# One condition for both matrices of a new expert, split by two engines, and one condition around the tail

## The chip, the cores and the metric

The program runs on one core of a Trainium2 chip. A core has TensorE (PE, matrix products; its weight loads are shown as PEld), VectorE (DVE), ScalarE (ACT), GpSimd (POOL) and SyncE (SP, which here issues most transfers). Each engine works through a list of its own in order and waits for the others by semaphores. The metric is the device time of one execution in microseconds (us). Three runs of the kernel before took 1461.64, 1463.62 and 1466.49 us; the median is 1463.62.

## The reference

Three stages follow each other: an attention with 32 landmarks, a mixture of eight experts of which each row takes one, and a feed-forward stage with a squared rectifier.

```python
x = attention(q, k, v)                       # 4608 rows of 512
logits = x @ w_gate; e = argmax(logits)      # one of 8 experts per row, gate_w its probability
for e in range(8):                           # w1[e] 512 x 1024, w2[e] 1024 x 512
    out[e's rows] = gate_w * (maximum(x[e's rows] @ w1[e], 0) @ w2[e])
h = maximum(out @ w_in, 0)                   # 512 x 2048
return (h * h) @ w_out                       # 2048 x 512
```

## The kernel before, in words

Only the middle stage, phase_m1, and its ends are touched. The rows were sorted by expert into tiles of 128 rows; tiles 0 and 1 are done earlier. The loop (from L1024) is written out for tiles 2 to 44, since 45 tiles would be needed for the worst distribution of rows; how many there are, `nt`, is known only on the chip. Tiles 36 (`NTF`) to 44 stand therefore each in a condition of its own, `tc.If(nt > j)` at L1031. A condition is a branch on every engine; the side that is not taken holds the instructions that bring each semaphore to the value it would have had, on POOL one INC_SWDGE_SEM for the tile's transfers.

A float32 matrix is held as the sum of two float16 matrices, a high and a low part, and each product is made of three: high by high, high by low, low by high. A tile `j` is one call of `step(j)`:

- mm1 in two halves of 48 matmuls each (L120 to L122): rows times w1. After each half ACT writes the high part of the hidden tile hT (L125) and DVE the low part (L126).
- mm2, 24 matmuls (L135): hT times w2. Its first four need the high part of the first half of hT, its next four the low part.
- post: the result is scaled and split (L143, L149, L157) and scattered by POOL (L158); prep of tile j + 2 (L56 to L94): the same for rows that POOL gathered (L80).
- the transpose of the next tile's rows, which SP issues as a transfer at the top of the step (L108) and which that tile's mm1 waits for.
- a part of a fill: one of 32 pieces of the last stage's weights, loaded by SP (L1055) and split by ACT, DVE and, for the second matrix, POOL (L1068 to L1095).

The experts' weights lie in `wb` (split) and the next expert's in `stg` (float32, 2 MB for each of w1 and w2). `change(j, i)` stands once for each matrix: `change(j, 0)` at the end of step j - 1, behind mm2, and `change(j, 1)` in step j between the two halves of mm1. Each has a condition (L966): where tile j begins a new expert, `conv` splits the staged matrix in four quarters, three by ACT (high, L1040) and DVE (low, L1049), one by POOL alone (L1042, L1046, L1047). Behind each condition SP issues the load of the matrix of the expert after that (L951), which does nothing where none is needed. With this input 38 tiles exist, and tiles 9, 14, 23 and 28 begin a new expert.

The last stage, phase_m2, takes blocks of 256 rows. Per block there are eight pairs: 24 matmuls (L1137 to L1139), then ACT, five DVE instructions on a tile `q` of eight slots, ACT and DVE again (L1142 to L1149). The products (L1161) of a block begin when the next block's second pair is out.

Of the kernel before, what the change touches and what calls it, by code (L numbers as in the profile page):

```python
# [6 lines left out]
F32 = mybir.dt.float32  # L7
# [19 lines left out]
NTL = 45  # L27
# [908 lines left out]
def phase_m1(tc, cst, x_rows, x2, w1, w2, rt, stg, wb, fill, first):  # L936
    nc = tc.nc
    identh = cst["identh"]
    with (
        tc.tile_pool(name="m1", bufs=1, reuse_waits="tile") as m1,  # L940
        tc.tile_pool(name="m2", bufs=2, reuse_waits="tile") as m2,
        tc.tile_pool(name="m3", bufs=3, reuse_waits="tile") as m3,
        tc.tile_pool(name="m5", bufs=5, reuse_waits="tile") as m5,
        tc.tile_pool(name="mph", bufs=2, space=PSUM, reuse_waits="tile") as mph,
        tc.tile_pool(name="mpy", bufs=2, space=PSUM, reuse_waits="tile") as mpy,
    ):
        st = [dict() for _ in range(NTL)]
# [14 lines left out]

        def change(j, i):

            s = st[j]
            with tc.If((chw[j // 16] >> (j % 16)) & 1):  # L966
                conv(nc, stg, wb, m2, i)
            load(s["nx"], s["ld"], i)

        pools = dict(xg=m3, xm=m3, s1=m5, xh=m2, gt=m5, xT=m2, hT=m1, yg=m1, ym=m3, s2=m3, ss=m3, xr=m2,  # L970
                     ph=mph, py=mpy)
# [18 lines left out]
        run(L.turn(st[PT]))  # L990
        change(PT, 0)
        idle = iter(())
# [5 lines left out]
        def step(j):  # L998
# [11 lines left out]
            run(L.mm1(st[j], 0))  # L1010
            change(j, 1)
            if j + 3 < NTL:
# [5 lines left out]
            if not last:  # L1018
                change(j + 1, 0)
            go(fl, old, pr, fl)  # L1020
            if j + 1 >= NTF:
                go(*(4 * [L.post(st[j], rt["sidx"][:, j:j + 1], rt["gidx"][:, j:j + 1])]))

        for j in range(PT, NTL):  # L1024
            if j + 2 < NTL:
                regs(j + 2)
            if j < NTF:
                step(j)
            else:

                with tc.If(nt > j):  # L1031
                    step(j)


def conv(nc, stg, wb, pool, i):

    for c in (3, 0, 1, 2):
        cs = slice(1024 * c, 1024 * c + 1024)
        if c < 3:
            nc.scalar.activation(wb[:, i, 0, cs], stg[:, i, cs], AF.Copy, scale=128.0)  # L1040
        if c == 3:
            nc.gpsimd.tensor_scalar(wb[:, i, 0, cs], stg[:, i, cs], 128.0, 1.0, op0=ALU.mult, op1=ALU.mult)  # L1042
            for h in range(2):
                hs = slice(cs.start + 512 * h, cs.start + 512 * h + 512)
                t = pool.tile([128, 512], F32, tag="cv", name="cv", bufs=1)
                nc.gpsimd.tensor_scalar(t, stg[:, i, hs], 128.0, 1.0, op0=ALU.mult, op1=ALU.mult)  # L1046
                nc.gpsimd.tensor_tensor(wb[:, i, 1, hs], t, wb[:, i, 0, hs], op=ALU.subtract)  # L1047
        else:
            nc.vector.scalar_tensor_tensor(wb[:, i, 1, cs], stg[:, i, cs], 128.0, wb[:, i, 0, cs],  # L1049
                                           op0=ALU.mult, op1=ALU.subtract)  # L1050

# [7 lines left out]
def wide_split(tc, pool, w, scale, dst, quad=None):  # L1059
# [17 lines left out]
    if quad is None:  # L1077
        to = c = g.bitcast(F32)
    else:
        if quad[1] == 0:  # L1080
            quad[0].append(pool.tile([128, 8, 256], F32, tag="fq", name="fq", bufs=1))
        c = quad[0][0]
        to = c[:, 4 + 2 * (1 - quad[1]):6 + 2 * (1 - quad[1])].rearrange("p s n -> p (s n)")
    V.scalar_tensor_tensor(to.bitcast(I32), hi, -0x80000000, g, op0=ALU.bitwise_and, op1=ALU.bitwise_or)
    if quad is not None:
        if quad[1] == 0:
            return

# [13 lines left out]

PRODS = ((6, 6, 0), (4, 4, 2), (1, 1, 0), (0, 0, 1), (2, 2, 0), (5, 3, 0), (3, 5, 1))

# [13 lines left out]
def phase_m2(tc, x2, wi, wo, wb, first, out):  # L1118
# [4 lines left out]
    with (  # L1123
# [7 lines left out]
        def pair(xT, hq, i):  # L1131
# [8 lines left out]

            q = n3.tile([128, 8, 128], F32, tag="q", name="q")
            ACT.activation(q[:, 4:8], ph.rearrange("p z (t n) -> p (z t) n", t=2), AF.Relu, scale=2.0 ** -7)  # L1142
            V.tensor_tensor(q[:, 4:8], q[:, 4:8], q[:, 4:8], op=ALU.mult)  # L1143
            V.tensor_tensor(q[:, 0], q[:, 7], q[:, 5], op=ALU.add)  # L1144
            V.tensor_tensor(q[:, 2], q[:, 6], q[:, 7], op=ALU.subtract)  # L1145
            V.tensor_tensor(q[:, 1], q[:, 0], q[:, 6], op=ALU.subtract)  # L1146
            V.tensor_tensor(q[:, 3], q[:, 4], q[:, 1], op=ALU.subtract)  # L1147
            ACT.activation(hq[:, 0, i], q[:, 0:7], AF.Copy, scale=0.5)  # L1148
            V.scalar_tensor_tensor(hq[:, 1, i], q[:, 0:7], 0.5, hq[:, 0, i], op0=ALU.mult, op1=ALU.subtract)  # L1149

# [140 lines left out]
```

## Time and profile before

| | us |
|---|---|
| median of three runs | 1463.62 |
| the profiled execution | 1462.96 |
| its span, from the first to the last instruction | 1461.3 |
| PE busy in the span | 1351.2 (92%) |
| DVE busy | 1020.3 (70%) |
| ACT busy | 569.7 (39%) |
| POOL busy | 319.6 (22%) |

All durations below are from the profiled execution, of which 1.7 us lie outside the span. The expert stage runs from about 287 to 717.5 us, the last stage from 736.2 us to the end. A tile of the expert stage is the stretch from its first mm1 matmul to the next tile's.

### The profile page before, as it was taken

Reading aid. Unit: us, or ns where it says so; the run is one execution under the profiler, and the core shown is the slowest. Engines: PE = TensorE matmul, PEld = TensorE weight load, DVE = VectorE, ACT = ScalarE, POOL = GpSimd, SP = SyncE. Lnnn points to the kernel's source line nnn. Section 1 sums busy time; section 2 is a strip of 40 time slices with the busy share of each in tenths; the row PEclk is TensorE's granted clock in tenths of the full one; section 3 lists DMA queues with packets and bytes.
Section 4 is the critical chain, followed back from the end, with each engine's and each line's share of the span. In section 5 each row is a group of like instructions: output and inputs, shape, how many; then the busy total and the mean of one; then the engine's idle time right before and its main releaser. Section 6 shows DMA issues by size and latency. Waiting matters only on the chain. (4 is left out here: it accounts for less than half of the span.)

```text
span 1461.3 us, 35927 instructions
## 1 busy us (share of the span) xinstructions
PE 1351.2 (92%) x14312; PEld 1077.3 (74%) x14312; DVE 1020.3 (70%) x2571; ACT 569.7 (39%) x989; POOL 319.6 (22%) x322
## 2 busy tenths in 40 slices
PE   5998889899898988799689999999999999999997
PEld 4555555667575766577477888888888888888886
DVE  6889998858989788988446655565555555556552
ACT  4555654324444443444223333333333333333331
POOL 4434652111533154633100000000000000000001
PEclk9989999999999999999889999999999999999999
DMA  8768663366658656344210111111111111101100
GB/s 197 174 154 192 166 156 107 124 171 131 202 117 219 146 143 173 91 124 110 56 31 1 30 30 30 31 30 30 30 30 30 30 30 23 24 17 28 30 16 30
DMA packets 133711, 127.23 MB, mean 87 GB/s; under 512 B 90832, under 2 KB 109264, under 8 KB 133520
## 3 DMA queue, kind: packets, MB, share of 16 engines
q1 hardware_dynamic: 123680, 94.45, 28.4%
q0 software_dynamic: 9200, 30.21, 6.8%
q8 instruction: 120, 1.97, 0.6%
q14 instruction: 71, 0.58, 0.1%
q10 hardware_dynamic: 640, 0.02, 0.0%
HBM read 217.39 MB, written 28.89 MB: 169 GB/s over the span
## 5 line engine op out<-in xcount | busy, mean ns | idle before, releaser
L1137 PE MATMUL h<-x2T,wi 128*128 128x256 f16 x1152 | 315.9, 274 | 18.8 <-PEq L1031 18.8
L1138 PE MATMUL h<-x2T,wi 128*128 128x256 f16 x1152 | 315.8, 274 | 0.0
L1139 PE MATMUL h<-x2T,wi 128*128 128x256 f16 x1152 | 315.7, 274 | 0.0
L135 PE MATMUL py<-wb,hT 128*128 128x512 f16 x864 | 201.8, 389 | 20.7 <-DVE hT L126 11.8
L122 PE MATMUL ph<-xT,wb 128*128 128x128 f16 x1152 | 197.1, 220 | 7.0 <-DVE wb L1049 6.3
L120 PE MATMUL ph<-xT,wb 128*128 128x128 f16 x1152 | 197.2, 220 | 6.8 <-DMA xT<-xh 4.3
L1143 DVE TENSOR_TENSOR q<-q 128x512 f32<-128x512 f32 x144 | 99.5, 691 | 142.5 <-ACT q L1142 142.5
L121 PE MATMUL ph<-xT,wb 128*128 128x128 f16 x1152 | 197.2, 220 | 0.0
L1171 POOL DMA_INDIRECT out<-out,fa x36 | 41.1, 1141 | 694.5 <-ACT out L1187 590.7
L1161 PE MATMUL o<-wo,wb 128*128 128x256 f16 x1512 | 176.4, 273 | 4.5 <-ACT wb L1148 3.2
L1161 PE MATMUL o<-wo,hq 128*128 128x256 f16 x1512 | 174.5, 273 | 0.6 <-ACT r L1167 0.6
L135 PEld LDWEIGHTS <-hT 128*128 128x128 f16 x864 | 83.8, 100 | 122.6 <-issue 14.7
L1161 PEld LDWEIGHTS <-wb 128*128 128x128 f16 x1512 | 147.8, 98 | 22.8 <-ACT wb L1148 3.7
L1142 ACT ACTIVATE q<-h 128x512 f32<-128x512 f32 x144 | 85.5, 594 | 195.5 <-PE h L1139 195.4
L1161 PEld LDWEIGHTS <-hq 128*128 128x128 f16 x1512 | 147.9, 98 | 17.8 <-issue 0.7
L1137 PEld LDWEIGHTS <-wi 128*128 128x128 f16 x1152 | 113.4, 98 | 32.9 <-issue 19.2
L1149 DVE SCALAR_TENSOR_TENSOR wb<-q,wb 128x896 f16<-128x896 f32 x72 | 78.6, 1092 | 73.6 <-ACT wb L1148 73.6
L120 PEld LDWEIGHTS <-wb 128*128 128x128 f16 x1216 | 120.3, 99 | 13.2 <-issue 4.9
L1149 DVE SCALAR_TENSOR_TENSOR hq<-q,hq 128x896 f16<-128x896 f32 x72 | 78.6, 1092 | 73.3 <-ACT hq L1148 73.3
L122 PEld LDWEIGHTS <-wb 128*128 128x128 f16 x1216 | 120.3, 99 | 8.0 <-DVE wb L1049 7.1
L1139 PEld LDWEIGHTS <-wi 128*128 128x128 f16 x1152 | 113.4, 98 | 13.7
L1138 PEld LDWEIGHTS <-wi 128*128 128x128 f16 x1152 | 113.4, 98 | 13.6
(296 smaller groups left out, 2251.4 us busy)
## 6 DMA issues: line engine op xcount, KB each, us to landing
stg<-in_moe_w SPq DMA_DIRECT2D x75, 2048.0 KB
qn<-in_q SPq DMA_DIRECT2D x16, 576.0 KB
kn<-in_k SPq DMA_DIRECT2D x16, 576.0 KB
vn<-in_v SPq DMA_DIRECT2D x16, 576.0 KB
fw<-in_moe_w_in SPq DMA_DIRECT2D x16, 512.0 KB
fw<-in_moe_w_out SPq DMA_DIRECT2D x16, 512.0 KB
x_rows<-xr SPq DMA_DIRECT2D x32, 192.0 KB
stg<-in_moe_w SPq DMA_DIRECT2D x16, 256.0 KB
```

What stands on the lines that cost most here:

```text
L120: nc.tensor.matmul(ph[:, f4], wh[:, c, fs], xT[:, c], start=(c == 0), stop=False)
L121: nc.tensor.matmul(ph[:, f4], wh[:, c, fs], xT[:, 4 + c], start=False, stop=False)
L122: nc.tensor.matmul(ph[:, f4], wl[:, c, fs], xT[:, c], start=False, stop=(c == 3))
L135: self.nc.tensor.matmul(py, hT[:, a, f], w[:, f], start=(i == 0), stop=(i == len(ps) - 1))
L1137: PE.matmul(ph[:, z], wi[:, 0, c, fs], xT[:, c], start=(c == 0), stop=False)
L1138: PE.matmul(ph[:, z], wi[:, 0, c, fs], xT[:, 4 + c], start=False, stop=False)
L1139: PE.matmul(ph[:, z], wi[:, 1, c, fs], xT[:, c], start=False, stop=(c == 3))
L1142: ACT.activation(q[:, 4:8], ph.rearrange("p z (t n) -> p (z t) n", t=2), AF.Relu, scale=2.0 ** -7)
L1143: V.tensor_tensor(q[:, 4:8], q[:, 4:8], q[:, 4:8], op=ALU.mult)
L1149: V.scalar_tensor_tensor(hq[:, 1, i], q[:, 0:7], 0.5, hq[:, 0, i], op0=ALU.mult, op1=ALU.subtract)
L1161: PE.matmul(po, hq[:, u, f, a], wo[:, x, f, w], start=(new and f == 0 and i == 0), stop=(f == 7 and i == 2), skip_group_check=True)
L1171: nc.gpsimd.indirect_dma_start(out=out, out_offset=bass.IndirectOffsetOnAxis(ap=fa[:, t, 2:4].bitcast(I32), axis=0), in_=s["out", t], in_o ...
```

## The change

There are four edits. `change(j)` is now one condition for both matrices, at the place of the old `change(j, 0)`: eight ACT and eight DVE instructions and none on POOL, then the two loads. `step` has no `change(j, 1)` any more. In the tail, tiles 36 and 37 keep their own conditions, and tiles 38 to 44 with theirs stand inside one more, `tc.If(nt > NTF + 2)`. The buffers are dealt out anew (three or four in place of two or three for several, one in place of two for xr), and the tile `q` of the last stage and the quad of the fills use seven slots in place of eight, one difference being written in place.

```diff
@@ -938,11 +938,11 @@
     identh = cst["identh"]
     with (
         tc.tile_pool(name="m1", bufs=1, reuse_waits="tile") as m1,
-        tc.tile_pool(name="m2", bufs=2, reuse_waits="tile") as m2,
         tc.tile_pool(name="m3", bufs=3, reuse_waits="tile") as m3,
-        tc.tile_pool(name="m5", bufs=5, reuse_waits="tile") as m5,
+        tc.tile_pool(name="m4", bufs=4, reuse_waits="tile") as m4,
+        tc.tile_pool(name="m5", bufs=7, reuse_waits="tile") as m5,
         tc.tile_pool(name="mph", bufs=2, space=PSUM, reuse_waits="tile") as mph,
-        tc.tile_pool(name="mpy", bufs=2, space=PSUM, reuse_waits="tile") as mpy,
+        tc.tile_pool(name="mpy", bufs=3, space=PSUM, reuse_waits="tile") as mpy,
     ):
         st = [dict() for _ in range(NTL)]
 
@@ -960,14 +960,16 @@
         def gather(j):
             L.gather(st[j], x_rows, rt["gidx"][:, j:j + 1])
 
-        def change(j, i):
+        def change(j):
 
             s = st[j]
             with tc.If((chw[j // 16] >> (j % 16)) & 1):
-                conv(nc, stg, wb, m2, i)
-            load(s["nx"], s["ld"], i)
-
-        pools = dict(xg=m3, xm=m3, s1=m5, xh=m2, gt=m5, xT=m2, hT=m1, yg=m1, ym=m3, s2=m3, ss=m3, xr=m2,
+                for i in range(2):
+                    conv(nc, stg, wb, i)
+            for i in range(2):
+                load(s["nx"], s["ld"], i)
+
+        pools = dict(xg=m4, xm=m3, s1=m5, xh=m3, gt=m5, xT=m3, hT=m1, yg=m1, ym=m3, s2=m3, ss=m3, xr=m1,
                      ph=mph, py=mpy)
         L = Layer1(nc, cst, wb, x2, lambda nm: mph.tile(*TILES[nm], tag="ph", name=nm) if nm == "pt" else pools[nm].tile(*TILES[nm], tag=nm, name=nm))
 
@@ -988,7 +990,7 @@
         for j in range(PT, PT + 2):
             run(L.prep(st[j]))
         run(L.turn(st[PT]))
-        change(PT, 0)
+        change(PT)
         idle = iter(())
         fls = [idle]
         def go(*gens):
@@ -1008,7 +1010,6 @@
                 first()
             go(po, pr, po, fl)
             run(L.mm1(st[j], 0))
-            change(j, 1)
             if j + 3 < NTL:
                 gather(j + 3)
             go(po)
@@ -1016,38 +1017,34 @@
             run(L.mm1(st[j], 1))
             run(L.mm2(st[j]))
             if not last:
-                change(j + 1, 0)
+                change(j + 1)
             go(fl, old, pr, fl)
             if j + 1 >= NTF:
                 go(*(4 * [L.post(st[j], rt["sidx"][:, j:j + 1], rt["gidx"][:, j:j + 1])]))
 
-        for j in range(PT, NTL):
-            if j + 2 < NTL:
-                regs(j + 2)
-            if j < NTF:
-                step(j)
-            else:
-
+        def some(js):
+
+            for j in js:
+                if j + 2 < NTL:
+                    regs(j + 2)
                 with tc.If(nt > j):
                     step(j)
 
-
-def conv(nc, stg, wb, pool, i):
-
-    for c in (3, 0, 1, 2):
+        for j in range(PT, NTF):
+            regs(j + 2)
+            step(j)
+        some(range(NTF, NTF + 2))
+        with tc.If(nt > NTF + 2):
+            some(range(NTF + 2, NTL))
+
+
+def conv(nc, stg, wb, i):
+
+    for c in range(4):
         cs = slice(1024 * c, 1024 * c + 1024)
-        if c < 3:
-            nc.scalar.activation(wb[:, i, 0, cs], stg[:, i, cs], AF.Copy, scale=128.0)
-        if c == 3:
-            nc.gpsimd.tensor_scalar(wb[:, i, 0, cs], stg[:, i, cs], 128.0, 1.0, op0=ALU.mult, op1=ALU.mult)
-            for h in range(2):
-                hs = slice(cs.start + 512 * h, cs.start + 512 * h + 512)
-                t = pool.tile([128, 512], F32, tag="cv", name="cv", bufs=1)
-                nc.gpsimd.tensor_scalar(t, stg[:, i, hs], 128.0, 1.0, op0=ALU.mult, op1=ALU.mult)
-                nc.gpsimd.tensor_tensor(wb[:, i, 1, hs], t, wb[:, i, 0, hs], op=ALU.subtract)
-        else:
-            nc.vector.scalar_tensor_tensor(wb[:, i, 1, cs], stg[:, i, cs], 128.0, wb[:, i, 0, cs],
-                                           op0=ALU.mult, op1=ALU.subtract)
+        nc.scalar.activation(wb[:, i, 0, cs], stg[:, i, cs], AF.Copy, scale=128.0)
+        nc.vector.scalar_tensor_tensor(wb[:, i, 1, cs], stg[:, i, cs], 128.0, wb[:, i, 0, cs],
+                                       op0=ALU.mult, op1=ALU.subtract)
 
 
 def wide_load(tc, pool, src, ncols):
@@ -1078,17 +1075,16 @@
         to = c = g.bitcast(F32)
     else:
         if quad[1] == 0:
-            quad[0].append(pool.tile([128, 8, 256], F32, tag="fq", name="fq", bufs=1))
+            quad[0].append(pool.tile([128, 7, 256], F32, tag="fq", name="fq", bufs=1))
         c = quad[0][0]
-        to = c[:, 4 + 2 * (1 - quad[1]):6 + 2 * (1 - quad[1])].rearrange("p s n -> p (s n)")
+        to = c[:, 5 - 2 * quad[1]:7 - 2 * quad[1]].rearrange("p s n -> p (s n)")
     V.scalar_tensor_tensor(to.bitcast(I32), hi, -0x80000000, g, op0=ALU.bitwise_and, op1=ALU.bitwise_or)
     if quad is not None:
         if quad[1] == 0:
             return
 
-        for o, x, y in ((0, 7, 6), (2, 5, 7), (1, 5, 0), (3, 4, 1)):
+        for o, x, y in ((0, 6, 5), (1, 4, 0), (2, 3, 1), (6, 4, 6)):
             P.tensor_tensor(c[:, o], c[:, x], c[:, y], op=ALU.subtract)
-        c = c[:, 0:7]
     yield
     nc.scalar.activation(dst[0], c, AF.Copy, scale=scale)
     yield
@@ -1100,7 +1096,7 @@
 
 TB = 256
 
-PRODS = ((6, 6, 0), (4, 4, 2), (1, 1, 0), (0, 0, 1), (2, 2, 0), (5, 3, 0), (3, 5, 1))
+PRODS = ((5, 5, 0), (3, 3, 2), (1, 1, 0), (0, 0, 1), (6, 6, 0), (4, 2, 0), (2, 4, 1))
 
 
 def load_block(nc, pool, x2, blk):
@@ -1138,15 +1134,15 @@
-            q = n3.tile([128, 8, 128], F32, tag="q", name="q")
-            ACT.activation(q[:, 4:8], ph.rearrange("p z (t n) -> p (z t) n", t=2), AF.Relu, scale=2.0 ** -7)
...
-            V.tensor_tensor(q[:, 2], q[:, 6], q[:, 7], op=ALU.subtract)
...
+            q = n3.tile([128, 7, 128], F32, tag="q", name="q")
+            ACT.activation(q[:, 3:7], ph.rearrange("p z (t n) -> p (z t) n", t=2), AF.Relu, scale=2.0 ** -7)
...
+            V.tensor_tensor(q[:, 6], q[:, 5], q[:, 6], op=ALU.subtract)
...
```

The first place is DVE between the two halves of a tile's hidden layer (hT is the hidden tile, xr the scattered result, wb the split weights). Before:

```order
L1071 TENSOR_SCALAR fm<-fw 128x512
L126 SCALAR_TENSOR_TENSOR hT<-ph,hT 128x512
L966 REGISTER_ALU x2
L966 COMPARE_AND_BRANCH
L1049 SCALAR_TENSOR_TENSOR wb<-stg,wb 128x1024 x3
L966 UNCONDITIONAL_BRANCH x2
L153 TENSOR_TENSOR ss<-s_5795,s_6581 128x1
L154 RECIPROCAL ss<-ss 128x1
L155 COPY xr<-gidx 128x1
L156 TENSOR_SCALAR xr<-ss 128x1
L157 SCALAR_TENSOR_TENSOR xr<-yg,s_6581,xr 128x512
L126 SCALAR_TENSOR_TENSOR hT<-ph,hT 128x512
```

The same place now, up to the next tile's condition:

```order
L1068 TENSOR_SCALAR fm<-fw 128x512
L126 SCALAR_TENSOR_TENSOR hT<-ph,hT 128x512
L153 TENSOR_TENSOR ss<-s_5675,s_6368 128x1
L154 RECIPROCAL ss<-ss 128x1
L155 COPY xr<-gidx 128x1
L156 TENSOR_SCALAR xr<-ss 128x1
L157 SCALAR_TENSOR_TENSOR xr<-yg,s_6368,xr 128x512
L126 SCALAR_TENSOR_TENSOR hT<-ph,hT 128x512
L966 REGISTER_ALU x2
L966 COMPARE_AND_BRANCH
L1046 SCALAR_TENSOR_TENSOR wb<-stg,wb 128x1024 x8
L966 UNCONDITIONAL_BRANCH x2
```

Three splits under a condition stood between the two writes of hT; they are gone there, and the condition behind the second write holds eight.

The second place is SP around the top of a step (stg is the staged next expert, fw a fill's piece, sc the loads' registers, xT the transposed rows). Before:

```order
L951 DMA stg<-in_moe_w 128x4x1024
L957 TENSOR_LOAD sc
L957 ISA x2
L958 TENSOR_LOAD sc
L958 ISA x2
L1055 DMA fw<-in_moe_w_in 128x1024
L108 DMA_TRANSPOSE xT<-xh 128x8x128
L966 REGISTER_ALU x2
L966 COMPARE_AND_BRANCH
L966 UNCONDITIONAL_BRANCH x2
L951 ISA
L951 DMA stg<-in_moe_w 128x8x512
```

The same place now:

```order
L951 DMA stg<-in_moe_w 128x4x1024
L951 ISA
L951 DMA stg<-in_moe_w 128x8x512
L957 TENSOR_LOAD sc
L957 ISA x2
L958 TENSOR_LOAD sc
L958 ISA x2
L1052 DMA fw<-in_moe_w_in 128x1024
L108 DMA_TRANSPOSE xT<-xh 128x8x128
```

The load of w2 (128x8x512) stood behind the transpose of the step and now stands ahead of it, right behind that of w1.

The third place is POOL at the last tiles of the tail (x2 is shown as x, the scatter's destination; an ISA row is the INC_SWDGE_SEM of a side that is not taken). Before, tile 43's end and tile 44's beginning:

```order
L1031 UNCONDITIONAL_BRANCH
L1031 ISA
L1031 UNCONDITIONAL_BRANCH
L1031 COMPARE_AND_BRANCH
L966 REGISTER_ALU x2
L966 COMPARE_AND_BRANCH
L1042 TENSOR_SCALAR wb<-stg 128x1024
L1046 TENSOR_SCALAR cv<-stg 128x512
L1047 TENSOR_TENSOR wb<-cv,wb 128x512
L1046 TENSOR_SCALAR cv<-stg 128x512
L1047 TENSOR_TENSOR wb<-cv,wb 128x512
L966 UNCONDITIONAL_BRANCH x2
```

Now, from tile 43's end to the first scatter of the last stage:

```order
L1030 UNCONDITIONAL_BRANCH
L1030 ISA
L1030 UNCONDITIONAL_BRANCH
L1030 COMPARE_AND_BRANCH
L158 DMA x_58<-xr,sidx 4736x1028
L1030 UNCONDITIONAL_BRANCH
L1030 ISA
L1030 UNCONDITIONAL_BRANCH
L1037 ISA
L1037 UNCONDITIONAL_BRANCH
L1167 DMA out<-out_14790,fa 4608x512
```

Each tile has kept its own ISA row, and the outer condition has one more behind them all, which alone is run where the outer condition is false.

## Rows read from the trace of the kernel before

**Rows 1.** Windows: stretch, its length, busy us (instructions) per engine, clock, DMA share, GB/s.

```profile
411.52:432.60 21.08, 21.08 (x242) 15.40 (x240) 17.03 (x42) 11.39 (x17) 6.52 (x6) 1.00 0.60 119
...
370.47:400.98 30.51, 24.16 (x241) 15.86 (x240) 29.25 (x58) 11.89 (x18) 15.28 (x13) 0.89 0.79 226
...
536.91:569.37 32.46, 24.10 (x242) 16.04 (x241) 29.89 (x53) 11.74 (x16) 22.12 (x18) 0.95 0.70 212
...
717.50:736.20 18.70, 0.00 (x0) 0.00 (x0) 2.47 (x9) 1.41 (x2) 0.97 (x1) 0.63 0.07 22
...
776.80:1430.00 653.20, 653.20 (x5985) 585.47 (x5984) 387.02 (x850) 228.90 (x334) 36.82 (x32) 1.00 0.12 26
```

**Rows 2.** Waits of PE from 286 to 720: total us, times, longest.

```profile
PE py L135 <- DVE hT L126: 11.8, 4, 5.7
```

**Rows 3.** Timeline of DVE in tile 9: start, us, instruction, [idle before, releaser].

```profile
367.07 5.63 DVE L1049 SCALAR_TENSOR_TENSOR wb<-stg,wb 128x1024 f16<-128x1024 f32 x3 [0.25 <-ACT wb L1040]
...
382.35 0.68 DVE L126 SCALAR_TENSOR_TENSOR hT<-ph,hT 128x512 f16<-128x512 f32 x1
...
382.95 3.48 DVE L1049 SCALAR_TENSOR_TENSOR wb<-stg,wb 128x1024 f16<-128x1024 f32 x3
```

**Rows 4.** Timeline of DVE in tile 10, where no matrix is split.

```profile
388.37 0.43 DVE L1073 TENSOR_SCALAR fg<-fg 128x512 f32<-128x512 f32 x1 [0.16 <-DVEq L966]
...
389.90 0.68 DVE L1095 SCALAR_TENSOR_TENSOR wi<-fg,wi 128x512 f16<-128x512 f32 x1
...
394.47 0.68 DVE L126 SCALAR_TENSOR_TENSOR hT<-ph,hT 128x512 f16<-128x512 f32 x1
```

**Rows 5.** Timeline of DVE in tile 23 and at the start of 24.

```profile
533.87 4.75 DVE L1049 SCALAR_TENSOR_TENSOR wb<-stg,wb 128x1024 f16<-128x1024 f32 x3
...
546.60 0.68 DVE L126 SCALAR_TENSOR_TENSOR hT<-ph,hT 128x512 f16<-128x512 f32 x1
...
556.89 2.02 DVE L1095 SCALAR_TENSOR_TENSOR wo<-fq,wo 128x1792 f16<-128x1792 f32 x1
```

**Rows 6.** Timeline of DVE in tile 28.

```profile
598.51 4.98 DVE L1049 SCALAR_TENSOR_TENSOR wb<-stg,wb 128x1024 f16<-128x1024 f32 x3 [0.25 <-ACT wb L1040]
...
614.48 0.68 DVE L126 SCALAR_TENSOR_TENSOR hT<-ph,hT 128x512 f16<-128x512 f32 x1
```

**Rows 7.** Line L1031 from 717 to 737: count, ns min/median/max, first and last start.

```profile
L1031 POOLq INC_SWDGE_SEM  x7: 1721/1733/1763, 721.9 to 734.6; - x7
...
L1031 PEldq COMPARE_BRANCH  x6: 2074/2932/3437, 717.7 to 733.1; - x6
```

**Rows 8.** Chain that ended last, 280 to 760: start, us, what.

```profile
738.32 0.21 PE h L1137
...
739.82 0.11 PE h L1137
```

**Rows 9.** Timeline of SP's issues, 372 to 393.

```profile
373.20 0.42 SPq L951 DMA_DIRECT2D stg<-in_moe_w  x1
...
380.27 1.28 SPq L108 DMA_TRANSPOSE xT<-xh  x1
...
386.65 1.91 SPq L951 DMA_DIRECT2D stg<-in_moe_w  x2
...
392.38 2.67 SPq L108 DMA_TRANSPOSE xT<-xh  x1
```

**Rows 10.** Timeline of PE at the start of tile 11.

```profile
400.98 0.22 PE L120 MATMUL ph<-xT,wb 128*128 128x128 f16 x1 [0.61 <-DMA xT<-xh]
```

**Rows 11.** Timeline of SP's issues, 282 to 310.

```profile
282.38 11.06 SPq L951 DMA_DIRECT2D stg<-in_moe_w  x3
...
295.17 3.08 SPq L108 DMA_TRANSPOSE xT<-xh  x1
...
300.24 0.91 SPq L951 DMA_DIRECT2D stg<-in_moe_w  x2
```

**Rows 12.** Timeline of PE at the start of tile 3.

```profile
307.24 0.22 PE L120 MATMUL ph<-xT,wb 128*128 128x128 f16 x1 [2.60 <-DMA xT<-xh]
```

More of the change, by code (lines that the diff above doesn't have):

```diff
@@ L1139, in pair @@
                     PE.matmul(ph[:, z], wi[:, 1, c, fs], xT[:, c], start=False, stop=(c == 3))
-            q = n3.tile([128, 8, 128], F32, tag="q", name="q")
-            ACT.activation(q[:, 4:8], ph.rearrange("p z (t n) -> p (z t) n", t=2), AF.Relu, scale=2.0 ** -7)
-            V.tensor_tensor(q[:, 4:8], q[:, 4:8], q[:, 4:8], op=ALU.mult)
-            V.tensor_tensor(q[:, 0], q[:, 7], q[:, 5], op=ALU.add)
-            V.tensor_tensor(q[:, 2], q[:, 6], q[:, 7], op=ALU.subtract)
[L1146 to L1149, printed above, removed]
+            q = n3.tile([128, 7, 128], F32, tag="q", name="q")
+            ACT.activation(q[:, 3:7], ph.rearrange("p z (t n) -> p (z t) n", t=2), AF.Relu, scale=2.0 ** -7)
+            V.tensor_tensor(q[:, 3:7], q[:, 3:7], q[:, 3:7], op=ALU.mult)
+            V.tensor_tensor(q[:, 0], q[:, 6], q[:, 4], op=ALU.add)
+            V.tensor_tensor(q[:, 6], q[:, 5], q[:, 6], op=ALU.subtract)
+            V.tensor_tensor(q[:, 1], q[:, 0], q[:, 5], op=ALU.subtract)
+            V.tensor_tensor(q[:, 2], q[:, 3], q[:, 1], op=ALU.subtract)
+            ACT.activation(hq[:, 0, i], q, AF.Copy, scale=0.5)
+            V.scalar_tensor_tensor(hq[:, 1, i], q, 0.5, hq[:, 0, i], op0=ALU.mult, op1=ALU.subtract)
         def product(b, k):
```

## The prediction

> **What bounds the kernel now.** I read the windows first, then PE's waits, the timelines of DVE and SP around a new expert, and the chain around the tail. The windows say that PE sets the pace: two plain tiles of the expert stage last 21.08 us and PE is busy through all of them, and in the last stage PE is busy for 653.20 of 653.20 us [rows 1]. So an edit moves the time only where PE stands still or runs at the lower clock. There are two such kinds of place. Two tiles that begin with a new expert last 30.51 us (tiles 9 and 10) and 32.46 us (23 and 24), which is 9.43 and 11.38 us over the plain pair; and between the stages PE does nothing for 18.70 us [rows 1].
>
> In a new expert's tile the largest wait of PE is for the low part of hT's first half: 11.8 us in four times [rows 2]. DVE writes it, and DVE works in order: in tile 9 it starts three splits of w1 at 367.07, then does fill, prep and post work, and comes to hT at 382.35 [rows 3]. DVE's queue, then, sets the end of such a tile. In the gap the six conditions shown take PE's sequencer 2.07 to 3.44 us each, one behind the other, and POOL pays 1.73 us seven times [rows 7].
>
> **The tail.** Seven skips in 18.70 us are 2.67 us each [rows 1]. The outer condition leaves one, so PE gets back 18.70 - 2.67 = 16.0 us; with the shortest and the longest skip of rows 7 for the one that is left, 16.6 and 15.3. The clock comes on top: the granted clock of the gap is 0.63, and PE's first matmuls of the last stage take 0.21 us, up to 738.32, where later ones take 0.11 [rows 1, 8]. From 736.2 to about 739.3 that is some 14 matmuls at 0.21, so 14 x 0.10 = 1.4 us. After a pause of 2.67 us in place of 18.70 I expect the higher of the two levels to stay; if it doesn't, the 1.4 is not won. What is late next is not in sight: the first pair's DVE and ACT chain starts behind PE's matmuls, and the transposes for the second block, which SP issues behind its own skips, come earlier by most of the gap too, since POOL does one INC_SWDGE_SEM for seven. **-17.4** (bounds -15.3 and -18.0).
>
> **The splits in DVE's queue.** After: eight splits in one go, at the place where three stood, and none behind hT's first write. Beside POOL's splitting three take 5.63 us (1.88 each) or 4.75 (1.58 each); without POOL three take 3.48, 1.16 each [rows 3, 5]. POOL has no share any more, so 8 x 1.16 = 9.3 us. Behind them comes the work up to hT, which in the undisturbed tile 10 lasts from 388.37 to 394.47, 6.10 us [rows 4]. The sum for tile 9 is 367.07 + 9.3 + 6.10 = 382.5, against 382.35 before [rows 3]: the longer row of splits is paid by the faster work behind it, +0.1. Tile 14 has the same order: +0.1. In the tile that follows each, a wait of 0.61 us for the transposed rows, late behind the load of w2 that now runs earlier, goes [rows 10]: -0.6 each. Both together **-1.0**.
>
> In tile 23 the fill has no L1095 in this place (0.68 less, [rows 4]): 533.87 + 9.3 + 5.4 = 548.6 against 546.60, hT 2.0 late [rows 5]. But no split of w2 stands behind it any more, where three with POOL beside would again take about the 4.75 of w1. PE needs after hT's low part 20 matmuls of 0.22 to 0.43 us, which are 4.4 to 8.6 us; I take 7.2, so that mm2 ends near 555.8 where the next tile began at 556.89, -1.1. Tile 24 then has the work of tile 23 no longer in DVE's queue, where L1095 of the second matrix (2.02 us) still stood at 556.89 [rows 5]; of the 32.46 - 30.51 = 1.95 us that this pair loses over the first [rows 1] I give back 1.5. **-2.6** (bounds: +1.5, if hT's delay is felt in full and little else comes back; -5, if the whole of the 2.02 and three splits' 3 us come back).
>
> In tile 28 L1095 is that of the second matrix, 2.02 instead of 0.68: 598.51 + 9.3 + 6.10 - 0.68 + 2.02 = 615.25, against 614.48 [rows 6]. **+0.8** (bounds -1 and +4, with splits at 1.58).
>
> ACT splits all eight high quarters ahead of the scaling of the previous tile's result, which comes later by as many splits; only DVE's post work, which stands behind DVE's own eight, needs it.
>
> **SP's queue.** This is the part that speaks against the change. Before, the transposes of tile 10's rows are issued at 380.27, behind the load of w1 (2 MB, 373.20), and tile 10 doesn't wait; the load of w2 is issued at 386.65, behind them, and tile 11's transposes (392.38) land behind it [rows 9, 10]. Now both loads stand ahead of tile 10's transposes. The load of w1 waits for DVE's fourth split, 367.07 + 4.64 = 371.7, that of w2 for the eighth, 376.4, when w1's is still in flight. At the start of the stage two such loads take from 282.38 to 300.24, when the next load, which waits for the second of them, is issued: 17.9 us, or 8.9 each [rows 11]. By these rows both have landed at 371.7 + 17.9 = 389.6, and the transposes can't be there before 1.28 us more (their issue in rows 9), 390.9. From the other side: from the issue of w2's load at 386.65 to tile 11's first matmul, held by the transposes, are 14.3 us [rows 9, 10]; with one load more ahead of it, 371.7 + 8.9 + 14.3 = 394.9. Tile 9 would end at 389.8 (its 389.7 before and 0.1), so tile 10 starts 1.1 to 5.1 us late. I take the middle, 3.1, because neither row is nearer: the start has more other transfers beside it, and the 14.3 has a fill's load in it, as the new order has. At tiles 9, 14 and 23 a load follows, behind 28 none: **+9.3** (bounds 0, if the loads leave engines free for the transposes, and 8.4 each, below).
>
> The Trainium skill, "DMA: Bandwidth & Descriptors", section "Queues, rings and completion order", has each ring of a DMA engine taken in its order, and this case's rows agree in kind: tile 11's transposes waited 0.61 us behind one load [rows 10]. By that rule the bound 0 would fall away and the sum would be between +3.3 and +15.3 for the three.
>
> At the start tile 3's transposes, issued at 295.17, hold tile 3 up by 2.60 us at 307.24 [rows 11, 12]. Now a load's issue that waits for the first w2 (300.24) stands ahead, so they go out at about 302, though with nothing of 2 MB before them. With the 8.6 us from 392.38 to 400.98 [rows 9, 10] they would release PE at 310.8, +3.6; since those 8.6 hold most of a load, I take **+1.0** (bounds 0 and +3.6).
>
> **What costs nothing.** The quads and `q` with seven slots: as many instructions, as wide, and PE is busy without a gap beside them [rows 1]. The conditions in plain tiles, one where two were: PE has no gap at either [rows 1]. The buffers: where more stand, nothing waited in the plain pair. The single xr: it is written once per tile, with POOL's scatter in between; should the write wait for the scatter, it would hold DVE's queue ahead of hT's second half, and a few tenths per tile would show at once in 36 tiles.
>
> **Sum.** -17.4 - 1.0 - 2.6 + 0.8 + 9.3 + 1.0 = -9.9. Against the profiled execution's own 1462.96 that is **1453.1 us**; this execution lies 0.66 under the median, which I leave as it is.
>
> **Rivals.** (1) Slower: the two loads hold the transposes fully. If these land as late after the loads' end as rows 9 and 10 have it after their issue, 389.6 + 8.6 = 398.2, each of three tiles starts 8.4 us late, 5.3 more than I took. A stop of that length has cost clock in tile 9: PE is busy 24.16 us in that pair for the work of 21.08, 3.1 more [rows 1]. So 1453.1 + 3 x (5.3 + 3.1) = 1478.3. From 4.8 us per change above my value it decides (the 9.9 of the sum and the 4.4 of the bound below, over three). For it speaks the order, against it that the loads are issued early in the tile, some 18 us before the need. Chance 0.06.
> (2) The slowness of the splits is not POOL's doing but that of ACT's beside it or of the transfers: eight cost 1.58 each as in rows 5, 3.4 us more in each of four changes: 1466.7. The undisturbed 1.16 had ACT beside it only in part. Chance 0.07.
> (3) One long jump costs as much as seven short ones, or the outer condition doesn't pass over all: the 17.4 stay lost, 1470.5. The skips' spread in rows 7 gives no sign that length of code is what counts. Chance 0.03.
> (4) More is won: the transposes find their way between the loads as in tile 10 before, which didn't wait: the 9.3 fall away, 1443.8. Chance 0.22.
> My forecast holds 0.62.
>
> **Range and chances.** About 0.3%, 4.4 us, is what this kernel's times can tell from no change. The forecast's own range, with 2 us either way per change in the transfers, is 1447 to 1460. To hold eight in ten it must take in most of (4): 1442; above, 1461 leaves out (1) to (3). Faster than 1458.6: nearly all of the forecast and (4), 0.82; within: (2) and the forecast's upper end, 0.10; slower: (1), most of (3), 0.08.
>
> **What would show it.** In the new trace the gap of PE between the stages should be one skip of 2 to 3.5 us, with the first matmuls at 0.11. In tiles 9, 14, 23 and 28 DVE should show eight splits at 1.16 us each in a row and come to hT's low part within a microsecond of before (2 later in 23), with no split behind. Tiles 10, 15 and 24 should begin with a wait for xT of about 3 us; none there means rival 4, over 8 means rival 1. Splits of over 1.5 us mean rival 2. If plain tiles are longer than 10.54 us, the buffers or conditions cost what I put at nothing, and the sum is wrong by that in 36 tiles.

## The result, and the profile after

The changed kernel takes 1451.67 us (median of 12 runs, 1448.39 to 1458.81), the kernel before 1464.22 (12 runs): a ratio of 0.9918, 95% interval 0.9900 to 0.9937, 12.5 us less. The forecast was 1453.1 us, faster. The profiled execution has a span of 1450.8 us against 1461.3, 10.5 less. Where they come from, by PE's matmuls in the two profiles:

| stretch | before | after | difference | forecast |
|---|---|---|---|---|
| up to tile 2 (nothing changed) | 291.7 | 288.5 | -3.2 | 0 |
| tiles 2 and 3 | 26.1 | 27.9 | +1.8 | +1.0 |
| tiles 9 and 10 | 30.5 | 30.2 | -0.3 | +2.6 |
| tiles 14 and 15 | 30.5 | 30.0 | -0.5 | +2.6 |
| tiles 23 and 24 | 32.5 | 37.7 | +5.2 | +0.5 |
| tiles 28 to 30 | 42.5 | 42.0 | -0.5 | +0.8 |
| gap between the stages | 18.7 | 5.0 | -13.7 | -17.4 |
| last stage | 725.1 | 725.8 | +0.7 | in the row above |

The total is right, and half of its terms are not. The first row is scatter between executions: the profiles below begin tile 2 at 288 to 293 us.

Windows of the changed kernel (stretch, its length, busy us and instructions of PE, PEld, DVE, ACT, POOL, then clock, DMA share, GB/s), to be read beside [rows 1]:

```profile
369.08:399.30 30.22, 24.43 (x241) 16.05 (x240) 25.99 (x60) 11.42 (x18) 3.99 (x4) 0.89 0.72 228
...
534.72:572.39 37.67, 26.15 (x241) 18.41 (x240) 27.91 (x59) 12.20 (x17) 7.22 (x9) 0.86 0.68 182
...
719.83:725.00 5.17, 0.16 (x1) 0.10 (x1) 2.47 (x9) 1.41 (x2) 0.97 (x1) 1.00 0.04 10
```

In tile 9's pair DVE is busy for 25.99 us where it was busy for 29.25, and POOL for 3.99 in place of 15.28, yet the pair is only 0.3 us shorter. The timeline of DVE in tiles 9 and 23, the counterpart of [rows 3, 5], shows why (start, us, instruction, [idle before, releaser]):

```profile
364.73 0.69 DVE L126 SCALAR_TENSOR_TENSOR hT<-ph,hT 128x512 f16<-128x512 f32 x1 [0.76 <-ACT hT L125]
365.67 9.17 DVE L1046 SCALAR_TENSOR_TENSOR wb<-stg,wb 128x1024 f16<-128x1024 f32 x8 [0.25 <-ACT wb L1045]
374.76 0.42 DVE L1070 TENSOR_SCALAR fg<-fg 128x512 f32<-128x512 f32 x1
...
380.86 0.69 DVE L126 SCALAR_TENSOR_TENSOR hT<-ph,hT 128x512 f16<-128x512 f32 x1
...
531.43 10.14 DVE L1046 SCALAR_TENSOR_TENSOR wb<-stg,wb 128x1024 f16<-128x1024 f32 x8 [0.17 <-issue]
...
546.99 0.68 DVE L126 SCALAR_TENSOR_TENSOR hT<-ph,hT 128x512 f16<-128x512 f32 x1
```

In tile 9 eight splits take 9.17 us and the work behind them, from 374.76, another 6.10, so that hT's low part begins 15.19 us after the first split; before it was 382.35 - 367.07 = 15.28 [rows 3]. The forecast had 15.4. In tile 23 it is 15.56 us, where it was 12.73 [rows 5]; the forecast had 14.7. PE waits for it in both tiles; in tile 9 the profile names L153, DVE's next instruction, which ends 0.06 us behind hT:

```profile
381.60 7.32 PE L135 MATMUL py<-wb,hT 128*128 128x512 f16 x20 [2.31 <-DVE ss L153]
...
547.73 6.18 PE L135 MATMUL py<-wb,hT 128*128 128x512 f16 x20 [4.87 <-DVE hT L126]
```

The gap is where the path was misjudged. The skipped branch of the outer condition on PE, ACT and POOL, from the view of its line (count, ns min/median/max, first and last start; ACT's EVENT_SEMAPHORE is the end of its jump):

```profile
L1037 PEldq COMPARE_BRANCH  x1: 3588/3588/3588, 718.2 to 718.2; - x1
...
L1037 ACTq COMPARE_BRANCH  x1: 45/45/45, 722.3 to 722.3; - x1
...
L1037 ACTq EVENT_SEMAPHORE  x1: 17/17/17, 724.9 to 724.9; - x1
...
L1037 POOLq INC_SWDGE_SEM  x1: 1768/1768/1768, 727.4 to 727.4; - x1
```

and the timelines of PE and of ACT behind it:

```profile
719.61 0.38 PE L135 MATMUL py<-wb,hT 128*128 128x512 f16 x1
725.00 0.27 PE L1133 MATMUL h<-x2T,wi 128*128 128x256 f16 x1 [5.01 <-ACTq L1037]
```

```profile
720.09 0.69 ACT L143 ACTIVATE yg<-py,gt 128x512 f32<-128x512 f32 x1 [3.35 <-PE py L135]
722.14 0.72 ACT L149 ACTIVATE xr<-yg,s 128x512 f16<-128x512 f32 x1 [1.37 <-DVE s L60]
729.49 0.60 ACT L1138 ACTIVATE q<-h 128x512 f32<-128x512 f32 x1 [6.62 <-PE h L1135]
```

PE's one skip takes 3.59 us and is over at 721.8, but its next matmul begins at 725.00 and was released by ACT's queue at the same line. ACT can't skip before it has issued tile 37's post work, at 722.14, so its jump begins at 722.3 and is over at 724.9. Seven skips hid that wait, one doesn't. And the clock falls even so: after three matmuls the chain of the changed kernel shows the long ones, and the granted clock from 725.56 to 729.00 is 0.54, near the lower of the two levels (1.2 of 2.4 GHz).

```profile
725.00 0.27 PE h L1133
725.56 0.21 PE h L1133
```

Of the transposes, tile 10's were in time and tile 24's were not. PE at the start of tiles 3 and 24:

```profile
304.21 0.22 PE L120 MATMUL ph<-xT,wb 128*128 128x128 f16 x1 [3.45 <-DMA xT<-xh]
...
559.15 0.27 PE L120 MATMUL ph<-xT,wb 128*128 128x128 f16 x1 [5.24 <-DMA xT<-xh]
```

### The profile page after: what moved, and what is told of

The parts are those of the page before. It is cut to its first block, busy times and chain, and to the rows that moved or that the text cites. A ratio compares the mean times of both kernels' runs of the same rounds, so it can differ in the third digit from the quotient of the medians.

```text
span 1450.8 us, 35065 instructions
## 1 busy us (share of the span) xinstructions
PE 1352.9 (93%) x14312; PEld 1080.1 (74%) x14312; DVE 1018.8 (70%) x2579; ACT 573.8 (40%) x997; POOL 260.6 (18%) x282
## 4 chain that ended last, share of the span: by engine, by line
PE 47%; DVE 2%; ACT 1%; issue 0%; DMA 0%; POOLq 0%; ACTq 0%
PE o L1157 22%; PE h L1133 8%; PE h L1135 8%; PE h L1134 8%; DVE wb L1145 1%; ACT wb L1144 1%; DVE q L1139 0%; DMA out<-out,fa 0%; DVE q L1143 0%; DVE q L1140 0%; DVE q L1141 0%; DVE q L1142 0%; POOLq L1283 0%; ACT q L1138 0%; ACT out L1183 0%
## 5 line engine op out<-in xcount | busy, mean ns | idle before, releaser
L120 PE MATMUL ph<-xT,wb 128*128 128x128 f16 x1152 | 200.8, 222 | 11.1 <-DMA xT<-xh 8.7
L122 PE MATMUL ph<-xT,wb 128*128 128x128 f16 x1152 | 200.8, 222 | 3.4 <-DVE wb L1046 3.2
L121 PE MATMUL ph<-xT,wb 128*128 128x128 f16 x1152 | 200.8, 222 | 0.0
L1157 PEld LDWEIGHTS <-wb 128*128 128x128 f16 x1512 | 147.8, 98 | 23.4 <-ACT wb L1144 4.4
L120 PEld LDWEIGHTS <-wb 128*128 128x128 f16 x1216 | 121.1, 100 | 16.7 <-issue 6.2
L1144 ACT ACTIVATE wb<-q 128x896 f16<-128x896 f32 x72 | 68.4, 950 | 147.4 <-DVE q L1143 147.4
L1144 ACT ACTIVATE hq<-q 128x896 f16<-128x896 f32 x72 | 68.4, 950 | 145.6 <-DVE q L1143 145.6
L1134 PEld LDWEIGHTS <-wi 128*128 128x128 f16 x1152 | 113.4, 98 | 16.7 <-issue 2.9
L1133 PEld LDWEIGHTS <-wi 128*128 128x128 f16 x1152 | 113.3, 98 | 16.1 <-SPq L1037 2.5
```

Source lines behind the costliest of these rows:

```text
L120: nc.tensor.matmul(ph[:, f4], wh[:, c, fs], xT[:, c], start=(c == 0), stop=False)
L121: nc.tensor.matmul(ph[:, f4], wh[:, c, fs], xT[:, 4 + c], start=False, stop=False)
L122: nc.tensor.matmul(ph[:, f4], wl[:, c, fs], xT[:, c], start=False, stop=(c == 3))
L1133: PE.matmul(ph[:, z], wi[:, 0, c, fs], xT[:, c], start=(c == 0), stop=False)
L1134: PE.matmul(ph[:, z], wi[:, 0, c, fs], xT[:, 4 + c], start=False, stop=False)
L1144: ACT.activation(hq[:, 0, i], q, AF.Copy, scale=0.5)
```

## The experiments

Each is the changed kernel with one edit, if not said otherwise; "before" was run beside each set on the same chip, and ratios are against it. In the table the last columns are from the profiles: PE's gap between the stages and the length of tiles 9 to 10 and 23 to 24. The gap is counted from 0.22 us behind the start of the last matmul, which is 0.16 us more than the idle time in the lines (5.01 for the change).

| kernel | median us | ratio, 95% interval | gap | 9, 10 | 23, 24 |
|---|---|---|---|---|---|
| the change | 1451.67 | 0.9918 (0.9900 to 0.9937) | 5.2 | 30.2 | 37.7 |
| the change, again | 1449.79 | 0.9901 (0.9881 to 0.9921) | 5.2 | 30.7 | 34.3 |
| no outer condition | 1465.74 | 1.0014 (0.9993 to 1.0034) | 17.7 | 29.9 | 34.6 |
| free banks | 1446.85 | 0.9885 (0.9866 to 0.9905) | 1.9 | 30.4 | 32.8 |
| POOL's share | 1464.45 | 1.0001 (0.9983 to 1.0020) | 5.3 | 34.0 | 35.0 |
| two conditions | 1437.16 | 0.9811 (0.9782 to 0.9841) | 5.1 | 27.5 | 27.2 |
| w2's load later | 1447.52 | 0.9890 (0.9872 to 0.9909) | 5.1 | 29.5 | 29.4 |
| old splits | 1456.50 | 0.9947 (0.9928 to 0.9967) | 5.3 | 30.8 | 32.7 |
| old splits, again | 1455.19 | 0.9944 (0.9919 to 0.9970) | 5.1 | 30.7 | 34.6 |
| lines exchanged | 1449.72 | 0.9905 (0.9878 to 0.9931) | 5.4 | 29.0 | 38.0 |
| three edits | 1433.48 | 0.9797 (0.9763 to 0.9831) | 1.9 | 27.7 | 27.6 |
| three edits, two xr | 1429.45 | 0.9754 (0.9728 to 0.9779) | 1.6 | 26.5 | 27.6 |
| split ahead of mm2 | 1465.70 | 1.0021 (0.9998 to 1.0045) | 1.2 | 29.4 | 29.6 |

**The outer condition taken out.**

```diff
-        some(range(NTF, NTF + 2))
-        with tc.If(nt > NTF + 2):
-            some(range(NTF + 2, NTL))
+        some(range(NTF, NTL))
```

> The changed kernel without the outer condition: tiles 38 to 44 each in a condition of their own again, all else as changed. Theory: the outer condition is nearly the whole gain; without it PE's gap between the stages goes back from 5.0 us to about 18.7 and the time is 13 to 14 us longer, about 1465. Rival: the new order of the splits carries the gain and the tail only a few us: 1452 to 1456.

The theory holds: 1465.74 us, and the gap is back at 17.66 us. With the new splits the condition around the tail is worth 14 to 16 us, and without it the change is not faster than before. Beside the old splits the same tail wins less, 7.5 to 8.0 us (below).

**Free PSUM banks for the last stage's first tiles.**

```diff
+        tc.tile_pool(name="mpd", bufs=3, space=PSUM, reuse_waits="tile") as mpd,
         tc.tile_pool(name="mph", bufs=2, space=PSUM, reuse_waits="tile") as mph,
...
+        for i in range(3):
+            mpd.tile([128, 512], F32, tag="pd", name="pd")
...
+        tc.tile_pool(name="nph", bufs=4, space=PSUM, reuse_waits="tile") as nph,
         tc.tile_pool(name="npo", bufs=1, space=PSUM, reuse_waits="tile") as npo,
-        tc.tile_pool(name="nph", bufs=4, space=PSUM, reuse_waits="tile") as nph,
```

> The changed kernel with the PSUM banks dealt out so that the first three h tiles of the last stage lie in banks which the expert stage does not use. Theory: PE, through with its jump 2.0 us after mm2, waits 3 us more because ACT, whose jump begins 2.3 us later behind its post work, has to bring the semaphore for a reused bank to its value; with free banks the gap is 2 to 2.5 us, the first ACT instruction of the stage comes 3 to 4 us earlier, and the time is 1447 to 1449. Rival: PE waits for ACT for another reason than the bank (weights, rows): gap 5.0 as before, 1451 to 1453.

PE and ACT at the beginning of the last stage, with free banks:

```profile
720.83 0.27 PE L1136 MATMUL h<-x2T,wi 128*128 128x256 f16 x1 [1.73 <-PEq L1040]
```

```profile
721.25 0.72 ACT L149 ACTIVATE xr<-yg,s 128x512 f16<-128x512 f32 x1 [1.37 <-DVE s L60]
724.04 0.60 ACT L1141 ACTIVATE q<-h 128x512 f32<-128x512 f32 x1 [2.07 <-ACTq L1040]
```

PE now waits for nothing but its own skip, begins at 720.83 while ACT is not yet through, and ACT's first relu comes 2.8 us after ACT's last post instruction where it came 7.35 after it. The wait was that for a bank whose last reader stands, by the program, in a tile that isn't run. The time, 1446.85 us, and the gap, 1.9 us, come out just below what was expected.

**POOL's quarter back, under the one condition.**

```diff
-                    conv(nc, stg, wb, i)
+                    conv(nc, stg, wb, m3, i)
...
+        if c == 3:
+            nc.gpsimd.tensor_scalar(wb[:, i, 0, cs], stg[:, i, cs], 128.0, 1.0, op0=ALU.mult, op1=ALU.mult)
```

(and the four other POOL instructions of the old `conv`.)

> The changed kernel, with both matrices under the one condition, but a quarter of each on POOL again (six DVE splits in place of eight; three buffers in place of four for xg). Theory: beside POOL a split takes DVE 1.6 to 1.9 us in place of 1.14, so six take as long as eight without POOL, 9.4 to 11 us, and the fill's work behind them is slowed too, by 2 to 3 us: 1454 to 1464. Rival: POOL's share frees DVE, and the slow splits of the kernel before had another cause: 6 x 1.14, 2.3 us less in each of four tiles: 1442 to 1445.

```profile
368.25 11.01 DVE L1054 SCALAR_TENSOR_TENSOR wb<-stg,wb 128x1024 f16<-128x1024 f32 x6 [0.25 <-ACT wb L1045]
387.76 0.68 DVE L126 SCALAR_TENSOR_TENSOR hT<-ph,hT 128x512 f16<-128x512 f32 x1
```

Six splits beside POOL take DVE 11.01 us, more than eight without it (9.17), and the work behind them 8.6 in place of 6.10: hT comes 19.5 us after the first split, not 15.2. The kernel takes 1464.45 us, half a us above what was expected. Rival 2 of the prediction falls: the slowness is POOL's. The Trainium skill, "SBUF — State Buffer", section "SBUF: two separate sides", has the ports that DVE and GpSimd share as an exclusive lock; that POOL slows DVE agrees, with 1.84 us per split in place of 1.15 beside POOL instructions of 1.1 to 2.0 us. Whether a split is held for the whole of such an instruction, these rows don't show.

**The split of w2 in its own condition again, without POOL.**

```diff
             run(L.mm1(st[j], 0))
+            change(j, 1)
...
-                change(j + 1)
+                change(j + 1, 0)
```

The load of w2 stands in `change(j, 1)` and moves with it, behind the transposes.

> The changed kernel with the split of w2 and its load in a condition of their own between the two halves of mm1 again, but still by ACT and DVE alone. Theory: hT's low part waits for all that stands ahead of it in DVE's queue; with four splits there in place of eight it comes 4 x 1.14 = 4.5 us earlier (376.3 in the times of the changed kernel's tile 9), mm2 then waits for the low quarters of w2 and ends 3 to 4 us earlier, in four tiles; and tile 24's transposes stand ahead of the load of w2. Sum -12 to -18: 1434 to 1440. Rival: the time of all eight splits is paid anyway, before hT or behind it, so a new expert's tile stays as long and only the transposes' wait goes: 1446 to 1450.

```profile
368.14 4.63 DVE L1045 SCALAR_TENSOR_TENSOR wb<-stg,wb 128x1024 f16<-128x1024 f32 x4 [0.25 <-ACT wb L1044]
378.79 0.68 DVE L126 SCALAR_TENSOR_TENSOR hT<-ph,hT 128x512 f16<-128x512 f32 x1
379.39 4.62 DVE L1045 SCALAR_TENSOR_TENSOR wb<-stg,wb 128x1024 f16<-128x1024 f32 x4
```

hT's low part comes 10.65 us after the first split in place of 15.19, the expected 4.5 us, and the kernel is 1437.16 us, within the expectation. So "both under one condition" is the costly part of this change: by the medians taking POOL out of the old order is worth 18.0 to 19.3 us (1455.19 and 1456.50 below with it), and setting both splits and both loads ahead gives 12.6 to 14.5 of them back. Of that the place of the load is 2.3 to 4.2 us, by the next run; the rest is the four splits ahead of hT.

**The load of w2 behind the transposes.** Both splits stay under one condition; only the load moves back to where it was, between mm1's halves.

```diff
             run(L.mm1(st[j], 0))
+            load(st[j]["nx"], st[j]["ld"], 1)
```

> The changed kernel with the load of w2 issued between the two halves of mm1 again, behind the next tile's transposes; both splits stay under one condition. Theory: the place of this load makes tile 24 (5.4 us in the profiled execution) and tile 3 (1.6 us) wait for their transposed rows; behind the transposes it costs nothing there, a few tenths at tiles 11, 16 and 25: 1446 to 1450. Rival: the late transposes of tile 24 come from the gathers running beside them and are there with any order of the loads: no change, 1451 to 1453.

Tiles 23 and 24 take 29.4 us; in the five profiles with both loads ahead and no splits on POOL (the change twice, no outer condition, free banks, lines exchanged) they take 32.8 to 38.0, and tile 24 waits 3.05 to 6.72 us for xT. The theory holds there and for the time, 1447.52.

The rival, POOL's gathers, has a part in it. In the changed kernel POOL issues two transfers in the second half of tile 9, but three in tile 23, since a gather there stands behind the fill's work on POOL:

```profile
383.00 0.99 POOL L158 DMA_INDIRECT x<-xr,sidx  x1 [16.49 <-DVE xr L157]
384.29 0.97 POOL L80 DMA_INDIRECT xg<-x_rows,gidx  x1 [0.30 <-issue]
```

```profile
546.92 1.00 POOL L80 DMA_INDIRECT xg<-x_rows,gidx  x1
549.13 0.99 POOL L158 DMA_INDIRECT x<-xr,sidx  x1 [1.22 <-DVE xr L157]
550.43 0.97 POOL L80 DMA_INDIRECT xg<-x_rows,gidx  x1 [0.30 <-issue]
```

The trace's DMA packets show how these meet the transposes. The 1024 packets of 256 bytes that are one tile's transposes begin as the loads end, 15.6 us after the start of tile 9 and 16.8 us after that of tile 23. In tile 9 they are through in 2.0 us, in tile 23 they take 6.7. The queues in the two stretches (384.5 to 386.7 and 551.3 to 558.3; q1 is SP's, q0 POOL's; packets, MB, share of 16 engines):

```profile
q1 hardware_dynamic: 1129, 0.50, 109.6%
q0 software_dynamic: 28, 0.12, 12.7%
```

```profile
q0 software_dynamic: 194, 0.66, 64.8%
q1 hardware_dynamic: 1157, 0.57, 48.3%
```

In those five profiles the transposes of tiles 10, 15 and 24 take 2.0 to 2.5 us beside at most 0.12 MB of POOL's, and the tile doesn't wait; beside 0.33 MB they take 3.3 us, with waits of 0.20 and 0.66; beside 0.49 to 0.68 MB they take 4.8 to 7.7 us, with waits of 2.58 to 6.72. With w2's load later they are through 13.9 us after the start of tile 23, ahead of POOL's first packet at 16.9. So the order of the loads makes the wait by pushing the transposes into POOL's transfers. No run moves POOL's transfers alone.

The theory fails at tile 3, which waits here too (5.4 us in this execution): tiles 2 and 3 vary from 25.1 to 30.5 us over the profiles, whatever the order.

**The change and its old splits, side by side.** The second kernel has `change(j, 0)`, `change(j, 1)` and the old `conv` again, with the tail, the PSUM buffers, the single xr and the seven slots of the change.

> The changed kernel with the old splits: two conditions per tile, a quarter of each matrix on POOL, the loads where they stood; tail, PSUM buffers and seven slots as changed, three buffers in place of four for xg for want of room. Theory: the new splits are worth next to nothing as a sum (shorter at tiles 9, 14 and 28 by 0.3 to 0.5 us each, longer at the start by 1.8 and at tile 24 by up to 5 when the transposes come late): 1448 to 1453. Rival: the splits without POOL are worth their shorter DVE time, 4 x 1 us or more: 1456 or above.

> The changed kernel once more, on one chip with its old splits. Theory: tile 24 waits 0 to 5 us for its transposed rows, by the execution, while tiles 9, 10, 14, 15 and 28 come out as in the first profile within 0.5 us; 1449 to 1454. Rival: the wait at tile 24 was that one execution's: tiles 23 and 24 back at 30 to 31 us.

> The kernel with the old splits again, beside the changed one on the same chip. Theory: what the new splits win and lose cancels, so it is within 3 us of the changed kernel. Rival: as in its first timed runs it is 4 to 5 us longer, then the new splits are worth that.

In the second profile of the change tile 24 waits 3.13 us, so the wait is not of one execution; tile 10 waits too, 0.66 us, and tiles 14 and 15 differ by 0.6 us from the first profile, a little more than expected. The old splits are slower twice, by 4.8 and 5.4 us of the medians; the theory that gains and losses cancel falls. In the two profiles taken side by side the new splits win 1.1 us in tiles 14 and 15, 1.7 in 28 to 30, 1.1 in tile 17, 0.9 at the start and 1.7 in the last stage, much of it no more than two executions differ by; most of the 1.1 in tile 17 is a wait of PE for POOL to reach the condition (0.95 us), which the kernel before doesn't have in that tile. It also stays open that the parts don't add up: the new splits with the old tail are 0.14% slower than before, the old splits with the new tail 0.53 to 0.56% faster, both together 0.82 to 0.99% faster.

**Two lines of a pair exchanged.**

```diff
-            V.tensor_tensor(q[:, 6], q[:, 5], q[:, 6], op=ALU.subtract)
             V.tensor_tensor(q[:, 1], q[:, 0], q[:, 5], op=ALU.subtract)
+            V.tensor_tensor(q[:, 6], q[:, 5], q[:, 6], op=ALU.subtract)
```

> The changed kernel with two lines of the last stage's pair exchanged, so that the difference written in place stands one instruction later. Theory: the in-place difference waits for the sum ahead of it, which reads the slot it writes, 0.12 us per pair; one instruction later nothing waits, the first block's pairs go from 3.89 to 3.77 us, 1.0 us in eight, and no more than 1 us behind that: 1450 to 1451, too little for the timed runs to tell, but plain in the trace. Rival: the 0.12 us are those of the changed slots' addresses: 3.89 as before.

The starts of two pairs in the chain, of the changed kernel, then with the lines exchanged:

```profile
734.16 0.61 DVE q L1139
...
738.05 0.61 DVE q L1139
```

```profile
730.95 0.61 DVE q L1139
...
734.72 0.61 DVE q L1139
```

3.89 us per pair against 3.77. The timed runs, 1449.72 us, can't tell so little. By DVE's starts, the difference into a slot of its own began 0.21 us after the sum ahead of it in the kernel before; in place, where it overwrites a slot that the sum reads, it begins 0.33 us after it. With the lines exchanged the four short instructions start 0.32, 0.21 and 0.21 us apart, where they were 0.33, 0.21 and 0.32: only one still stands right behind an instruction that it depends on.

**Three edits together, then with two xr buffers.** Two conditions, free banks and the exchanged lines; the second kernel has `xr=m2` with two buffers (and three for xg) as well.

> Three edits together on the changed kernel: the split of w2 by ACT and DVE in a condition of its own between the halves of mm1, free PSUM banks for the first h tiles of the last stage, and the exchanged lines in a pair. Theory: the three act at different places and add up: 14 us at the new experts, 3 to 4 at the gap, 1 in the first block, so 1430 to 1436. Rival: w2's split ends behind hT as late as before; then only the bank, the transposes and the pairs count, 1442 to 1446.

DVE in tile 17 of the first:

```profile
475.40 0.15 DVE L155 COPY xr<-gidx 128x1 int32<-128x1 int32 x1 [4.86 <-DMA x<-xr,sidx]
```

The three add up, but DVE waits 4.86 us for the scatter of the tile before, and tile 17 takes 16.39 us. POOL issues that scatter at 467.39, after SP's transposes of the last stage's first block out of the same tensor (458.97 to 463.50); that it waits for these is read from the order, not tested.

> The three edits together with two buffers for xr as in the kernel before (and three for xg). Theory: in the profile of the three edits tile 17 lasts 16.39 us in place of 10.54, since DVE must wait with xr for the scatter before, which waits until the last stage's first block has been transposed; a second xr takes that away: 3 to 6 us less, 1428 to 1431. Rival: DVE's wait is for another thing than xr's scatter, or is that execution's alone: 1432 to 1434, tile 17 over 11 us.

With two buffers tile 17 takes 10.54 us and the kernel 1429.45, as expected: 20.3 us less than the changed kernel on the same chip, ratio 0.9754 to before.

**The split of w2 ahead of mm2.** The kernel with two xr, `change(j, 1)` moved behind the second half of mm1.

> As the kernel before this one, but the split of w2 behind the second half of mm1, ahead of mm2. Theory: hT's second low part no longer stands behind the four splits, but mm2's first matmuls wait for ACT's high quarters of w2, which now start behind the second half: within 2 us of it either way. Rival: the second low part sets the end of mm2, so 1 to 2 us less in each of four tiles: 4 to 8 us less.

Both the theory and the rival fall: 1465.70 us, 36 more than the kernel with two xr. PE's waits in the expert stage (total us, times, longest):

```profile
PE py L135 <- ACTq L969: 27.8, 30, 2.1
PE py L135 <- ACT wb L1047: 18.1, 4, 5.0
```

Every plain tile now takes 11.43 us or more in place of 10.54. mm2 reads what a condition may have written, so PE waits until ACT has come to that condition, whose false side brings the semaphore to its value; and ACT comes to it behind hT's second half. Where the condition stood before, ACT was there in time.

## Why the prediction was right, and where it was wrong

- **DVE's queue sets a new expert's tile: right**, in the trace (15.19 us against 15.4) and by both experiments on it (POOL's share and two conditions). Rival 2 was wrong.
- **The tail: the right mechanism, mis-sized**, -13.7 where it said -17.4. The step that failed is "What is late next is not in sight". ACT's skip was: it begins 2.3 us behind the end of mm2, by the post work, is over 3.1 us behind PE's, and PE's matmul waits for it. PE's own skip took 3.59 us where the mean of the seven was 2.67. The 1.4 us of the clock were not won, since 5.01 us of pause still bring the half level; with free banks and a gap of 1.9 us the gap's clock cost is gone too.
- **The transfers: mis-sized in both directions.** The sum had 3.1 us for each of three tiles. In the change's two profiles tile 10 waits 0 and 0.66 us, tile 15 not at all, tile 24 5.24 and 3.13 us: for the first two the forecast's lower bound was nearly true, for the last more than its middle. By the Trainium skill, "DMA: Bandwidth & Descriptors", section "Queues, rings and completion order", each ring is taken in its order; this agrees here, where the transposes' packets begin as the loads end, 15.6 us after the start of tile 9 and 16.8 after that of tile 23. What the sum lacked is POOL's transfers, beside which the transposes of tile 24 took 6.7 us in place of 2.0. The clock behind the stop was missing too, though rival 1 counts it: tile 24 takes 13.24 us at a granted clock of 0.78 where a plain tile takes 10.54.
- **Tile 23: the term was right, and a wait hid it.** Of the -2.6, tile 23 itself was to give 1.1 and tile 24 1.5. In the changed kernel mm2 of tile 23 ends 19.2 us after the tile's start, where the tile took 19.98; with w2's load later, where tile 24 doesn't wait, tile 23 is 1.1 us and tile 24 1.9 us shorter than before. The wait for the transposes and the clock behind it turned this into +5.2.
- **"Costs nothing": wrong in one item.** The seven-slot `q` costs 0.12 us per pair while the chain binds, 1.0 us in the first block. The single xr made DVE wait nowhere in the change's two profiles, but for 0.7 to 2.5 us in all with two conditions and for 5.4 us with the three edits.
- **The total was right by cancelling, which is luck.** The gap with the last stage (4.4 us), tile 24 (4.7) and the start (0.8) missed by 9.9 us one way; tiles 9 and 14 (2.9 and 3.1), tile 28 (1.3) and the scatter ahead of tile 2 (3.2) by 10.5 the other.

## What to carry to other kernels

An engine works through its list in order, so a piece of work that is made cheaper and moved ahead of what the critical engine waits for can cost as much as before: count everything that stands ahead of that one instruction, and move behind it what can wait. A skipped condition costs each engine its own jump, and a wait that crosses it is over only when the engine waited for has jumped too; here free buffers took that wait off the path. And data that a condition may have written makes its reader wait for the condition itself, so where the condition stands in the writer's list matters even in the tiles in which it is false.

## What the runs showed of the hardware that was not expected

One jump over the seven tiles took PE 3.59 us, a little over the longest of the single ones (3.44), and POOL's one INC_SWDGE_SEM took 1.77 us. A pause of PE of 5.01 us brought the lower clock three matmuls later, and one of 5.03 us in the second profile from the first matmul on, while after a pause of 1.73 us the matmuls came every 0.11 us. The packets of one tile's transposes (128x1024 f16) took 2.0 to 2.5 us beside at most 0.12 MB of POOL's transfers and 4.8 to 7.7 us beside 0.49 to 0.68 MB. A difference written in place, right behind the instruction that reads its slot, began 0.33 us after it and not 0.21, which costs DVE 0.12 us.
